# A cached-attention decode block on one core: the last row's second layer in two groups, tail loads first, zero matmuls between

## The chip, the cores and the metric

The kernel runs on one core of a Trainium2 chip. The metric is the device time of one execution in microseconds (us). TensorE is PE in the profile, its weight loads are PEld, VectorE is DVE, ScalarE is ACT, GpSimd is POOL and SyncE, which issues most loads, is SP.

## The reference

Eight rows (one token each, 448 wide) go through attention over a cached window, a dense block with silu, and both once more with the same weights and the same cache:

```python
def _A_ref(x, k_cache, v_cache, wq, wo):
    W = min(4096, max(256, Sk // 4))            # 1024
    q = (x @ wq).reshape(B, Sq, Hq, Dh).transpose(0, 2, 1, 3)   # 16 heads of 256
    k = jnp.repeat(k_cache[:, :, Sk - W:, :], 2, axis=1)        # 8 key heads
    v = jnp.repeat(v_cache[:, :, Sk - W:, :], 2, axis=1)
    p = _softmax(jnp.einsum("bhqd,bhkd->bhqk", q, k) * (Dh ** -0.5), axis=-1)
    o = jnp.einsum("bhqk,bhkd->bhqd", p, v)
    return o.transpose(0, 2, 1, 3).reshape(B, Sq, Hq * Dh) @ wo
...
x = x + _A_ref(_layernorm(x), A_k_cache, A_v_cache, A_wq, A_wo)
x = x + _B_ref(_layernorm(x), B_w1, B_w2)       # silu(x @ w1) @ w2
x = x + _A_ref(_layernorm(x), A_k_cache, A_v_cache, A_wq, A_wo)
x = x + _B_ref(_layernorm(x), B_w1, B_w2)
```

Each row has its own 8 key and 8 value heads of 1024 x 256 in bf16 (512 KB each), 64 MB over all rows.

## The kernel before, in words

Every K and V head of a row is loaded once and serves both layers. It lands in one of 30 slots in SBUF (`load_kv`, L495); the sequence is K of row 0, V of row 0, K of row 1 and so on. SP issues a load as soon as the slot's last reader is done; from the 31st load on that reader is the second layer of a row two places back. The weights come in between: wq (three full chunks, L435, and two 64-partition tails, L429) first, w2 (L453) and wo (L447) after the first row's K, w1 (L441) after the first row's V, with two 64-partition tails of its own (L429).

A row's first layer: DVE turns each K slot in place by 32x32 blocks (`transposes`, L638). PE takes the scores of four key heads at a time (`scores`, L654), so that two passes of 32 matmuls give all 16 heads in one bank. `softmax` (L669 to L683) takes the maximum of each partition on DVE, exchanges it between the partitions that belong to one head by an ACT step (L670), a matmul against a fixed pattern (L671) and a minimum on DVE (L673), then the exp on ACT (L674), a permutation on PE (L676) and a 32x32 turn on DVE (L678). `products` (L689) and, for the last two heads that land, `products_late` (L698) multiply with V; `o_turn` (L711, L715, L719) divides by the sum and turns the result to columns; `wo_rows` (L740) applies wo; `fold` (L746, L528, L531) adds it to the row. `chain(b)` is the dense block (L751 statistics input, L757, L543 for w1, L778 tanh, L798 for w2) and the projection to the second layer's q (L813, L818, L819, L826, L830). The second layer runs `attend2` and `values2` on the slots that are still there.

In the second layer of rows 0 to 6, wo, the dense block and the output are done for all seven rows at once (`final_rows`, L864 to L908). Row 7 goes alone to its end (`final_last`, to L945), after all loads.

The program is a list of tasks with declared reads and writes (`Plan`); the order of the tasks on PE, DVE, ACT and POOL is a table written out in the file (`ORDER`, L13), and SP's order is that of the program text. Each engine takes its tasks strictly in that order and waits by semaphores for tasks of other engines. A load with `via="act"` is issued by ACT ahead of all its tasks.

Of the kernel before, what the change touches and what calls it, by code (L numbers as in the profile page):

```python
# [4 lines left out]
BF16 = mybir.dt.bfloat16  # L5
# [29 lines left out]
    "dve":  # L35
# [14 lines left out]
    "act":  # L50
# [8 lines left out]
    "pool":  # L59
        "0 1 79 130 131 250 219 249 236 378 348 379 365 507 508 477 494 636 606 637 623 765 735 752 766 895 894 864 "  # L60
        "881 993 1024 1023 1010 1108 1125 1162 1218",
}


class Task:
    __slots__ = ("eng", "fns", "dur", "row", "name", "deps", "idx", "end", "sem", "val", "vc", "users", "via")

    def __init__(self, eng, fns, dur, row, name):
        self.eng, self.fns, self.dur, self.row, self.name = eng, fns, dur, row, name
        self.deps = {}  # L70
        self.users = 0
        self.end = None

# [148 lines left out]
def bass_interleave_layers__sliding_block_cached__dense_activation_silu__decode_kernel(  # L222
# [9 lines left out]
    P = 128  # L232
# [833 lines left out]
```

## Time and profile before

| | us |
|---|---|
| median of 3 runs | 235.23 |
| the three runs | 236.98, 235.23, 233.61 |
| the profiled execution | 233.86 |
| its span, first to last instruction | 232.0 |
| PE busy (matmuls) | 161.9 |
| DVE busy | 154.6 |
| ACT busy | 71.8 |
| POOL busy | 22.8 |

The span was executed at a mean granted TensorE clock of 0.963 of full speed. The page divides the span into 40 slices of 5.8 us and gives in each the busy share in tenths; a row of the timeline gives start, length, engine, line, operation, what is written and read, the count of instructions, and in brackets how long the engine had been idle and what released it. HBM read was 77.67 MB.

### The profile page before, as it was taken

How to read it: one execution, taken by the hardware profiler on the slowest of the kernel's cores; microseconds unless marked ns; L12 is line 12 of the kernel's file. 1: busy time of each engine (PE TensorE's matmuls, PEld its weight loads, DVE VectorE, ACT ScalarE, POOL GpSimd, SP SyncE). 2: the span in 40 equal slices, each digit the busy share in tenths (PEclk: the TensorE clock that was granted, in tenths of full speed). 3: DMA queues.
4: the chain of work that ended last, by engine and by line, in shares of the span. 5: the costliest groups of instructions: out<-in, count | busy, mean ns of one | idle time of the engine just before them, and what ended most of it. 6: DMA issues, size and time to landing. Idle time of an engine off the chain costs nothing.

```text
span 232.0 us, 7993 instructions
## 1 busy us (share of the span) xinstructions
PE 161.9 (70%) x3558; PEld 90.8 (39%) x3558; DVE 154.6 (67%) x361; ACT 71.8 (31%) x218; POOL 22.8 (10%) x41
## 2 busy tenths in 40 slices
PE   0000617174777889798697988897987999899883
PEld 0000604022434455345443554454444445444542
DVE  6108999996894796488559935793985599424413
ACT  2000070663103341342243222413622441343241
POOL 1000201003000120030011001010200020000020
PEclk9999999679589999999999988999999999999999
DMA  6999999999999999999999999999999999700000
GB/s 213 296 386 410 383 381 394 405 415 420 403 410 383 411 407 375 381 414 406 353 384 413 408 374 410 386 357 395 412 410 393 386 399 410 284 3 3 3 3 4
DMA packets 22680, 78.19 MB, mean 337 GB/s; under 512 B 2279, under 2 KB 5302, under 8 KB 22262
## 3 DMA queue, kind: packets, MB, share of 16 engines
q1 hardware_dynamic: 22326, 76.93, 85.5%
q10 hardware_dynamic: 320, 0.75, 1.2%
q8 instruction: 28, 0.46, 0.8%
q14 instruction: 6, 0.05, 0.1%
HBM read 77.67 MB, written 0.01 MB: 335 GB/s over the span
## 4 chain that ended last, share of the span: by engine, by line
PE 39%; SPq 20%; DVE 15%; DMA 13%; ACT 8%; issue 3%; DVEq 0%
DMA slot<-in_A_k_cache_dram 13%; SPq L495 11%; PE bank L654 9%; DVE slot L638 8%; SPq L447 7%; PE bank L689 7%; PE pair L740 4%; PE pair L813 3%; PE bank L813 2%; PE pair L798 2%; ACT ot L711 2%; PE bank L826 2%; ACT ot L746 1%; PE pair L528 1%; DVE q1s L669 1%
## 5 line engine op out<-in xcount | busy, mean ns | idle before, releaser
L638 DVE STREAM_TRANSPOSE slot<-slot 128x512 uint32<-128x512 uint32 (+1 forms) x96 | 81.0, 870 | 19.2 <-DMA slot<-in_A_k_cache_dram 18.6
L654 PE MATMUL bank<-slot,qbd 128*16 128x256 bf16 (+1 forms) x1024 | 39.0, 286 | 5.5 <-POOL qbd L625 1.9
L689 PE MATMUL bank<-slot,qbd 128*24 128x512 bf16 (+6 forms) x440 | 34.1, 405 | 3.1 <-DVE qbd L678 2.3
L654 PEld LDWEIGHTS bank<-slot,qbd 128*16 128x16 bf16 (+1 forms) x1024 | 23.4, 88 | 14.3 <-ACT qbd L830 4.3
L762 POOL TENSOR_TENSOR fcols<-fcols 128x1 f32<-128x1 f32 x17 | 9.4, 552 | 87.1 <-ACT fcols L760 79.3
L625 POOL TENSOR_TENSOR qbd<-q1s,fcols 128x256 bf16<-128x256 bf16 x16 | 9.7, 612 | 84.0 <-PE bank L698 37.5
L711 ACT ACTIVATE ot<-bank,q1s 128x512 bf16<-128x512 f32 x16 | 11.0, 686 | 18.7 <-PE bank L689 15.5
L740 PE MATMUL pair<-wo_sb,q1s 128*1 128x449 bf16 x288 | 16.1, 353 | 0.6 <-ACT wo_sb L483 0.4
L830 ACT ACTIVATE qbd<-bank 128x256 bf16<-128x256 f32 x16 | 6.1, 383 | 33.5 <-PE bank L826 33.5
L597 PE MATMUL pair<-slot,wq_sb 128*128 128x16 bf16 x128 | 3.6, 174 | 16.8 <-DVE slot L590 16.8
L689 PEld LDWEIGHTS bank<-slot,qbd 128*24 128x24 bf16 (+6 forms) x440 | 10.1, 93 | 11.6 <-DVE qbd L678 3.7
L669 DVE TENSOR_REDUCE q1s<-bank 128x1 f32<-128x256 f32 x16 | 6.8, 423 | 10.3 <-PE bank L654 10.2
L471 DVE TENSOR_REDUCE slot<-wo_sb 128x6 f32<-128x2688 bf16 x4 | 11.7, 2924 | 0.0
L678 DVE STREAM_TRANSPOSE qbd<-bank 128x256 bf16<-128x256 bf16 x16 | 7.5, 466 | 6.3 <-PE bank L676 6.1
L479 ACT ACTIVATE slot<-w_sb 128x448 bf16<-128x448 bf16 x6 | 3.5, 576 | 24.4 <-DMA w_sb<-in_B_w_dram 24.2
L670 ACT ACTIVATE q1s<-fcols,q1s 128x4 f32<-128x4 f32 x16 | 4.7, 296 | 19.1 <-DVE q1s L669 19.1
L674 ACT ACTIVATE qbd<-bank,q1s 128x256 bf16<-128x256 f32 x16 | 7.6, 472 | 8.8 <-DVE q1s L673 8.6
L813 PE MATMUL pair<-wq_sb,q1s 128*1 128x256 bf16 x256 | 9.8, 293 | 0.6 <-ACT q1s L804 0.6
L751 DVE TENSOR_TENSOR q1s<-pair,fcols 128x5 bf16<-128x5 f32 x17 | 2.7, 159 | 11.2 <-PE pair L531 11.1
L597 PEld LDWEIGHTS pair<-slot,wq_sb 128*128 128x128 bf16 x128 | 3.5, 104 | 16.9 <-DVE slot L590 16.9
L671 PE MATMUL bank<-q1s,quad 128*128 128x4 f32 x32 | 6.1, 262 | 5.5 <-ACT q1s L670 5.3
L798 PE MATMUL pair<-w_sb,q1s 128*1 128x449 bf16 x112 | 7.4, 353 | 3.6 <-DVE q1s L786 3.4
(158 smaller groups left out, 240.0 us busy)
## 6 DMA issues: line engine op xcount, KB each, us to landing
slot<-in_A_k_cache_dram SPq DMA_DIRECT2D x64, 512.0 KB, 8.7
slot<-in_A_v_cache_dram SPq DMA_DIRECT2D x64, 512.0 KB, 9.7
wo_sb<-in_A_wo_dram SPq DMA_DIRECT2D x4, 896.0 KB, 15.0
wq_sb<-in_A_wq_dram SPq DMA_DIRECT2D x3, 1024.0 KB, 10.6
w_sb<-in_B_w_dram SPq DMA_DIRECT2D x1, 1568.0 KB, 19.8
w_sb<-in_B_w_dram SPq DMA_DIRECT2D x1, 1344.0 KB, 17.4
wq_sb<-in_A_wq_dram ACTq DMA_DIRECT2D x2, 256.0 KB, 6.0
w_sb<-in_B_w_dram ACTq DMA_DIRECT2D x1, 128.0 KB, 9.9
```

Source lines behind the costliest of these rows:

```text
L447: dma(lambda e, g=g: e.dma_start(wo_sb[:, 4 * g * PW:4 * (g + 1) * PW].rearrange("p (h n) -> p h n", n=PW)[:, :, R0:M1], A_wo[1024 * g:102 ...
L471: dve(lambda e, rows=rows, s=s: e.tensor_reduce(s, rows[:, :, R0:M1].rearrange("p c (a n) -> p c a n", a=2), AX.X, ALU.add, negate=True), ...
L495: dma(lambda e: e.dma_start(slots[s][:, :].rearrange("p (u d) -> p u d", d=DH), cache[b, kvh, S0:SK, :].rearrange("(p u) d -> p u d", p=P) ...
L625: pool(lambda e, k2=k2: e.tensor_tensor(qdata(0, k2), q1s[:, b, 64 * k2:64 * k2 + 64].rearrange("p (n r) -> p n r", r=2).unsqueeze(3) .bro ...
L638: dve(lambda e, v=v: e.transpose(v, v), keys, keys, 0.15 + n / 2 / 950, b, ("KW%d" if n > 1024 else "KT%d") % k)
L654: fns.append(lambda e, w=w, j=j, kv=kv, cb=cb, par=par: e.matmul(sc[32 * j:32 * j + up_to, 0:256], w, kv, start=(cb == 0 and par == 0), st ...
L689: pe([lambda e, t=t: e.matmul(bank[ob][32 * t:32 * t + m, :], pT_sb[L][:, 64 * t:64 * t + m], v[:, 512 * t:512 * t + 512], start=True, sto ...
L711: act(lambda e: e.activation(o_t, src[1], ACTF.Copy, scale=sm[b][:, 4 * L + 3:4 * L + 4]), bk(src[0]) + [("sm", b, L, 3)], okey, 0.62, b, ...
L740: fns.append(lambda e, i=i, w=w, c0=c0: e.matmul(bank[XB][32 * (i % 4):32 * (i % 4) + 1, c0:c0 + D + 1], oT[:, oT_col(i):oT_col(i) + 1], w ...
L762: pool(lambda e: e.tensor_tensor(rhalf, var4, nhalf, ALU.pow), ["var4", "nhalf"], ["rhalf"], 0.54, b, "pow" + name)
L798: fns.append(lambda e, f=f, w=w, c0=c0: e.matmul(bank[XB][32 * (f % 4):32 * (f % 4) + 1, c0:c0 + D + 1], hT[b][:, f:f + 1], w, start=(f < ...
L813: pe([lambda e, j=j, c=c, qh=qh, k2=k2, h=h, n=n: e.matmul(qh[32 * j:32 * j + 1, :], xbt[b][:, xcol(c, k2):xcol(c, k2) + 1], view(wq_sb[:] ...
```

## The change

Four things are edited, and all four order tables are new.

1. *Tails first.* `load_tails()` is called before `load_wq()`, so that the tails of wq and w1 stand ahead of the full chunks of wq. Of each pair of tails one goes on SP's queue, the other on ACT's.
2. *Table first.* In ACT's order the load of the activation tables (task 2) moves from the last row's part to the first place.
3. *Zero matmuls.* `warm(b, n)` adds n rounds of four matmuls with a weight column of zeros and 512 columns of wq, one in each column group, into the bank of the first layer's products. There are 8 rounds ahead of row 0's products, and 12, 5, 4, 4, 4, 4, 4 and 3 declared after the products of rows 0 to 7; the first stands at the head of PE's order, and all read wq.
4. *Two groups.* The second layer of row 7 is done for key heads 0 to 3 and 4 to 7 separately, each with its own score bank, softmax, products, `o_turn` and half of wo. The maximum of a group is exchanged between partitions by two 32x32 turns and a small minimum on DVE in place of the ACT and PE steps. The batch of seven rows uses another bank for w1 (`WB8`).

```diff
+    WARM = (8, 12, 5, 4, 4, 4, 4, 4, 3)
...
-                    [(key, 3 + h)], 64 * n * 2, "%st%d" % (key, h), rate=400e3, via="act")
+                    [(key, 3 + h)], 64 * n * 2, "%st%d" % (key, h), rate=370e3, via=("sp", "act")[h])
...
     def load_wq():
...
-            if c == 0:
-                load_tails()
...
-    def softmax(b, L):
+    def softmax(b, L, part=None):
+        sb, n, m = (SC[L], L, L) if part is None else (part[0], part[1], 1 - part[1])
...
+            mt, mg = part[2][:, 0:64].bitcast(F32), part[2][:, 64:80].bitcast(F32)
+            bias = mt[:, 0:1]
+            dve(lambda e: e.tensor_reduce(mt[:, 0:1], x, AX.X, ALU.max, negate=True), bk(sb), [("mt", n)] + part[3], 0.41,
+                b, "max%d" % L)
+            dve(lambda e: e.transpose(mt, mt), [("mt", n)], [("mt", n)], 0.21, b, "mT")
+            dve(lambda e: e.tensor_reduce(mg, mt.rearrange("p (n q) -> p n q", q=4), AX.X, ALU.min), [("mt", n)],
+                [("mg", n)] + part[3], 0.17, b, "mg")
+            dve(lambda e: e.transpose(mt.rearrange("p (n q) -> p n q", q=4), mg.unsqueeze(2).broadcast_to([P, 8, 4])),
+                [("mg", n)], [("mt", n), K[1]], 0.21, b, "mb")
...
+    def warm(b, n):
+        for k in range(n):
+            pe([lambda e, i=i: e.matmul(bank[OB[0]][32 * i:32 * i + 1, :], zero_b, wq_sb[:, 512 * i:512 * i + 512],
+                                        start=True, stop=True, tile_position=(0, 32 * i), skip_group_check=True)
+                for i in range(4)], WQ_R + ["cols0"], bk(OB[0]), 0.054, b, "fill")
...
-        XB8, YB8, WB8 = SC[0], OB[0], LB[0]
+        XB8, YB8, WB8 = SC[0], OB[0], SC[0]
...
+    load_tails()
     load_wq()
...
+        if b == 0:
+            warm(b, WARM[0])
         for kvh in range(HKV - LATE):
             products(b, 0, kvh, OB[0])
         o_turn(b, 0, (OB[0], bank[OB[0]][:]), ot[:], ["ot"], 2 * LATE, H, oT1[b], [("oT1", b, 0)], "0")
+        warm(b, WARM[b + 1])
...
     def attend2(b):
+        if b == LAST:
+            s = slot_of[LAST - 1, "v", 2]
+            for k2, sb in enumerate((SC[1], OB[1])):
+                scores(b, 1, k2, sb)
+                softmax(b, 1, (sb, 1 - k2, slots[s][:, 128 * k2:128 * k2 + 128], slot_key(s)))
+            return
...
+        s = slot_of[LAST - 1, "v", 2]
+        for k2, ob in enumerate((SC[1], OB[1])):
+            for kvh in range(4 * k2, 4 * k2 + 4):
+                products_late(b, kvh, bank[ob][:, 0:256], bk(ob), k2, "PVL")
+            o_turn(b, 1 - k2, (ob, bank[ob][:, 0:256]), slots[s][:, 512:768] if k2 else ot[:, 0:256],
+                   slot_key(s) if k2 else ["ot"], 8 - 8 * k2, 16 - 8 * k2, oT2[b], [("oT2", k2)], "L")
+            wo_rows(b, range(16 * k2, 16 * k2 + 16), oT2[b], [("oT2", k2)], "woL", NCH - 4)
+        fold(b, 1.0, [], "L")
```

In the new orders the tasks of rows 1 to 6 keep nearly their sequence on PE, with the zero rounds between them; DVE's order at the start and in row 0 differs more. The last row's groups stand on PE as: scores of both, half of w1 and the statistics of the batch, products of group one with the permutation of group two between, products of group two, then the turns and wo of both. ACT has the two copies (L711 before) one after the other and then the two turned copies (L719 before).

More of the change, by code (lines that the diff above doesn't have):

```diff
@@ L639, in transposes, with scores @@
                 ("KW%d" if n > 1024 else "KT%d") % k)
-    def scores(b, layer, k2):
-        sc = bank[SC[layer]]
+    def scores(b, layer, k2, sb=None):
+        sb = SC[layer] if sb is None else sb
+        sc = bank[sb]
         q = qbd[layer][:]
@@ L657, in scores @@
             pe(fns, [x for j in range(4) for x in slot_key(slot_of[b, "k", 4 * k2 + j])] + [("pad", layer)] + QB(layer, k2),
-               bk(SC[layer]), 0.0285, b, "S%d.%d" % (layer, k2))
-    def softmax(b, L):
-        lb = bank[LB[L]]
-        x = bank[SC[L]][:, 0:256]
+               bk(sb), 0.0285, b, "S%d.%d" % (layer, k2))
+    def softmax(b, L, part=None):
+        sb, n, m = (SC[L], L, L) if part is None else (part[0], part[1], 1 - part[1])
+        lb = bank[LB[n]]
+        x = bank[sb][:, 0:256]
@@ L664, in softmax @@
         px = lb[:, 256:512]
-        mneg, bias, acc, rlr = (sm[b][:, 4 * L + i:4 * L + i + 1] for i in range(4))
-        mq = sm[b][:, 8 + 4 * L:12 + 4 * L]
-        K = [("sm", b, L, i) for i in range(5)]
+        mneg, bias, acc, rlr = (sm[b][:, 4 * n + i:4 * n + i + 1] for i in range(4))
+        mq = sm[b][:, 8 + 4 * n:12 + 4 * n]
+        K = [("sm", b, n, i) for i in range(5)]
         mx, lr = lb[:, C_MX:C_MX + 4], lb[:, C_L:C_L + 1]
-        dve(lambda e: e.tensor_reduce(mneg, x, AX.X, ALU.max, negate=True), bk(SC[L]), [K[0]], 0.41, b, "max%d" % L)
@@ L670, in softmax @@
-        act(lambda e: e.activation(mq, sel4, ACTF.Copy, scale=mneg), [K[0], "sel4"], [K[4]], 0.2, b, "mq%d" % L)
-        pe(lambda e: e.matmul(mx, quad[:], mq, start=True, stop=True, skip_group_check=True), [K[4], "quad"], bk(LB[L]),
-           0.2, b, "mx%d" % L)
-        dve(lambda e: e.tensor_reduce(bias, mx, AX.X, ALU.min), bk(LB[L]), [K[1]], 0.15, b, "mb%d" % L)
-        act(lambda e: e.activation(e_sb[L], x, ACTF.Exp, bias=bias, scale=1.0, accum_out=acc),
-            bk(SC[L]) + [K[1]], EK[L] + [K[2]], 0.6, b, "exp%d" % L)
@@ L676, in softmax @@
-        pe(lambda e: e.matmul(px, perm[:], e_sb[L], start=True, stop=True),
-           EK[L] + PERM + QM * L, bk(LB[L]), 0.13, b, "perm%d" % L)
-        dve(lambda e: e.transpose(view(pT_sb[L], 0, [(64, 4), (1, 2), (2, 32)]), px.bitcast(BF16)[:, 1:512:2]),
-            bk(LB[L]), PT[L], 0.44, b, "turn%d" % L)
+        if part is None:
+            dve(lambda e: e.tensor_reduce(mneg, x, AX.X, ALU.max, negate=True), bk(sb), [K[0]], 0.41, b, "max%d" % L)
+            act(lambda e: e.activation(mq, sel4, ACTF.Copy, scale=mneg), [K[0], "sel4"], [K[4]], 0.2, b, "mq%d" % L)
+            pe(lambda e: e.matmul(mx, quad[:], mq, start=True, stop=True, skip_group_check=True), [K[4], "quad"],
+               bk(LB[n]), 0.2, b, "mx%d" % L)
+            dve(lambda e: e.tensor_reduce(bias, mx, AX.X, ALU.min), bk(LB[n]), [K[1]], 0.15, b, "mb%d" % L)
+        else:
+            mt, mg = part[2][:, 0:64].bitcast(F32), part[2][:, 64:80].bitcast(F32)
[7 more added lines that the diff above has]
+                [("mg", n)], [("mt", n), K[1]], 0.21, b, "mb")
@@ L680, in softmax @@
+        act(lambda e: e.activation(e_sb[m], x, ACTF.Exp, bias=bias, scale=1.0, accum_out=acc),
+            bk(sb) + [K[1]], EK[m] + [K[2]], 0.6, b, "exp%d" % L)
+        pe(lambda e: e.matmul(px, perm[:], e_sb[m], start=True, stop=True),
+           EK[m] + PERM + QM * m, bk(LB[n]), 0.13, b, "perm%d" % L)
+        dve(lambda e: e.transpose(view(pT_sb[m], 0, [(64, 4), (1, 2), (2, 32)]), px.bitcast(BF16)[:, 1:512:2]),
+            bk(LB[n]), PT[m], 0.44, b, "turn%d" % L)
         pe([lambda e, t=t: e.matmul(lr[32 * t:32 * t + 32, :], lsel[:], acc, start=True, stop=True,
@@ L681, in softmax @@
                                     tile_position=(0, 32 * t), skip_group_check=True) for t in range(4)],
[L682 to L683 removed]
+           [K[2], "lsel"], bk(LB[n]), 0.05, b, "l%d" % L)
+        dve(lambda e: e.reciprocal(rlr, lr), bk(LB[n]), [K[3]], 0.15, b, "rl%d" % L)
     def products(b, L, kvh, ob):
@@ L998, in values2 @@
     def values2(b):
-        end = HKV if b < LAST else HKV - LATE
-        for kvh in range(end):
-            products(b, 1, kvh, OB[1])
-            freed.add((b, "v", kvh))
-        pump()
-        o_turn(b, 1, (OB[1], bank[OB[1]][:]), ot[:], ["ot"], 2 * (HKV - end), H, oT2[b], [("q1s", b)], "1")
-        if b == LAST:
-            for i in range(0, 4 * end, 8):
-                wo_rows(b, range(i, i + 8), oT2[b], [("q1s", b)], "woL")
-            late(b, 1, oT2[b], "oT2")
-            wo_rows(b, range(NCH - 4 * LATE, NCH), oT2[b], [("oT2", b, 7)], "woL7")
-            fold(b, 1.0, [], "L")
+        if b < LAST:
+            for kvh in range(HKV):
+                products(b, 1, kvh, OB[1])
+                freed.add((b, "v", kvh))
+            pump()
+            o_turn(b, 1, (OB[1], bank[OB[1]][:]), ot[:], ["ot"], 0, H, oT2[b], [("q1s", b)], "1")
+            return
+        s = slot_of[LAST - 1, "v", 2]
[6 more added lines that the diff above has]
+        fold(b, 1.0, [], "L")
     pump()
```

20 lines of the change are left out of this document (9 added, 11 removed), and 86 rows, old and new, of the table ORDER.

## The prediction

> **What bounds the kernel now.** I read the page's 40 slices first, then busy time by stretch (columns: stretch, its length, busy time and instruction count of PE, weight load, DVE, ACT and POOL, granted clock, DMA share, GB/s).
>
> ```profile
> PEclk9999999679589999999999988999999999999999
> DMA  6999999999999999999999999999999999700000
> GB/s 213 296 386 410 383 381 394 405 415 420 403 410 383 411 407 375 381 414 406 353 384 413 408 374 410 386 357 395 412 410 393 386 399 410 284 3 3 3 3 4
> ```
>
> ```profile
> 2.00:6.00 4.00, 0.38 (x5) 0.28 (x5) 3.16 (x18) 1.47 (x2) 0.00 (x0) 1.00 0.96 329
> 6.00:9.00 3.00, 0.48 (x12) 0.40 (x12) 1.12 (x6) 0.05 (x1) 0.00 (x0) 1.00 1.04 242
> 9.00:13.00 4.00, 0.00 (x0) 0.00 (x0) 0.00 (x0) 0.00 (x0) 0.00 (x0) 1.00 1.03 346
> 13.00:17.00 4.00, 0.00 (x0) 0.00 (x0) 0.00 (x0) 0.00 (x0) 0.00 (x0) 1.00 0.99 400
> 56.00:86.00 30.00, 21.77 (x440) 11.75 (x444) 22.79 (x43) 8.67 (x27) 3.11 (x6) 0.89 1.02 404
> 86.00:96.00 10.00, 8.34 (x187) 5.11 (x180) 5.99 (x15) 2.57 (x9) 0.55 (x1) 1.00 0.97 375
> 111.00:119.00 8.00, 6.16 (x133) 3.65 (x135) 3.29 (x9) 2.79 (x8) 0.02 (x1) 1.00 0.99 352
> 86.00:201.00 115.00, 98.14 (x2157) 54.73 (x2153) 81.68 (x174) 38.27 (x115) 12.03 (x21) 0.99 1.01 393
> ```
>
> The span falls in two: 203 us (35 slices of 5.8) in which the DMA engines are hardly ever idle, then 29 us without loads, which is one row's dependent chain. No engine is full in the first part; the loads are. So the time is the moment when the last V slot lands, plus the tail. When it lands, and why the stream isn't always at 404 GB/s, is in the SP queue: who made it wait (us in total, times, longest), then the last two V loads, and the loads from 60 to 80.
>
> ```profile
> SPq L495 <- PE bank L654: 56.9, 15, 11.5
> ```
>
> ```profile
> L495 SPq DMA_DIRECT2D slot<-in_A_v_cache_dram x2: 327/380/434, 195.8 to 196.1; - x2
> ...
> DMA to landing us min/median/max: 6.0/6.4/6.9
> ```
>
> ```profile
> L495 SPq DMA_DIRECT2D slot<-in_A_v_cache_dram x3: 327/328/434, 68.6 to 79.9; - x3
> ...
> DMA to landing us min/median/max: 4.5/7.0/9.6
> ```
>
> The last load lands at 196.1 + 6.9 = 203.0, so the tail is 232.0 - 203.0 = 29.0. SP waits for the score matmuls of layer 2 (L654), which free the K slots; once for 11.5 us, up to the first gate at 68.6. The load that lands soonest after its issue does so in 4.5 us: a queue of three or four transfers, since a 512 KB slot takes 1.3 at 404. Behind such gates the stream sags: (404-375)/404 x 10 = 0.7 us lost in 86 to 96, (404-352)/404 x 8 = 1.0 in 111 to 119, and 3.1 over the 115 us from 86.
>
> **Part 1: tails first.** Before, 736 KB of 64-partition loads on ACT's queue (columns: count, KB each, us to landing) mix with the three 1 MB loads of wq on SP's.
>
> ```profile
> wq_sb<-in_A_wq_dram ACTq DMA_DIRECT2D x2, 256.0 KB, 6.0
> w_sb<-in_B_w_dram ACTq DMA_DIRECT2D x1, 128.0 KB, 9.9
> w_sb<-in_B_w_dram ACTq DMA_DIRECT2D x1, 96.0 KB, 11.0
> ```
>
> ```profile
> L435 SPq DMA_DIRECT2D wq_sb<-in_A_wq_dram x3: 369/422/851, 1.2 to 2.1; - x3
> ...
> DMA to landing us min/median/max: 6.8/10.6/13.0
> ```
>
> wq is complete at 2.1 + 13.0 = 15.1. Against 400 GB/s the stretches lose 3 x (400-242)/400 = 1.2 us, 4 x (400-346)/400 = 0.5 and 4 x (400-329)/400 = 0.7, together 2.4. Afterwards the tails go two and two on SP and ACT ahead of wq, and mix mostly with each other. If they move at the worst rate seen, 736 KB take 3.1 us at 242 against 1.9 at 400: a loss of 1.2 in place of 2.4. I take 1.2 us off every later landing. Bounds: 2.4 if nothing is lost, 0 if the same packets are as slow in any order, and 0.8 worse, because SP issues wq behind two more issues of some 0.4 us. [...] The 242 while two queues mix speaks for a cost of mixing, which an order can change.
>
> **Part 2: table first, and a zero round at the head of PE.** The table load moves ahead of an ACT wait that has slack in both orders: nothing. But the first PE instruction now waits for all five wq loads, at 13.9 by part 1. Behind it in PE's queue stand the transposition of x, the statistics and q1; DVE, ACT and POOL wait for those. Before, that early chain had come to its DVE step by 7.4:
>
> ```profile
> 7.23 0.17 DVE L564 TENSOR_SCALAR slot<-bank 128x8 f32<-128x8 f32 x1
> ```
>
> after which DVE waited for K, transposed, and only then let q1 go:
>
> ```profile
> 17.63 2.53 DVE L638 STREAM_TRANSPOSE slot<-slot 128x1024 uint32<-128x1024 uint32 x2 [10.23 <-DMA slot<-in_A_k_cache_dram]
> ```
>
> ```profile
> 23.87 3.58 PE L597 MATMUL pair<-slot,wq_sb 128*128 128x16 bf16 x128 [16.84 <-DVE slot L590]
> ```
>
> The chain is at most 7.4 long, so it ends by 13.9 + 7.4 = 21.3, and the cover is K transposes. In DVE's new order the last piece ahead of q1 stands behind four wide transposes and a half (4.5 x 1.27, from about 16, with the waits for K and small pieces: near 24), before behind three, at 23.9. So q1 keeps its time and DVE is ahead by one and a half. Cost 0; without that cover up to 1, taken up by DVE's row sums.
>
> **Part 3: 48 zero rounds.** Each is four matmuls of 512 columns in four column groups. The nearest rows are L689 with few weight columns, alone and three sets in a row:
>
> ```profile
> 200.50 0.39 PE L689 MATMUL bank<-slot,qbd 128*24 128x512 bf16 x4
> ```
>
> ```profile
> 205.33 0.82 PE L689 MATMUL bank<-slot,qbd 128*12 128x512 bf16 x12
> ```
>
> A round is (0.82-0.39)/2 = 0.21 us, alone 0.39; 48 are 10 us of PE. Twenty lie in row 0 and its chain, where PE waits for DVE and DMA and the granted clock falls to a half (the 6, 7, 5 and 8 of the slices). The last q projection of row 0, right ahead of the scores that open the gate at 68.6, and the same in row 7:
>
> ```profile
> 63.58 1.92 PE L813 MATMUL bank<-wq_sb,q1s 128*1 128x512 bf16 x16
> ```
>
> ```profile
> 191.96 1.08 PE L813 MATMUL bank<-wq_sb,q1s 128*1 128x512 bf16 x16
> ```
>
> That is 0.84, and the other half of the projection, as many columns, lies in the same dip: 1.7 together. At full clock, and with part 1, the gate opens some 3 us sooner while the loads move by 1.2: the queue is one or two transfers deeper. I count the sag of 86 to 96 as gone and 0.4 of the next, 1.1 us. Bounds: 3.1 (all of it) and 0. The other 28 rounds, three to five a row, stand mostly before a matmul that waits: the statistics for DVE, the two softmax steps for ACT, the fold for the row copy. For the last, in row 1:
>
> ```profile
> 85.04 0.29 PE L528 MATMUL pair<-cols,ot 128*128 128x1 bf16 x5 [0.73 <-ACT ot L746]
> ```
>
> Two rounds, 0.42, fit into 0.73. I charge 0.3 for a few that don't fit. The bound is two rounds of each row's chain uncovered, 0.42 in each of seven rows, 2.9 us; below nothing is excluded beyond the clock gain, as they compute nothing that is used. [...]
>
> **Part 4: the last row in two groups** (and the batch's w1 in another bank, no cost). Now its last scores end at 216.70 and the exp starts at 218.18:
>
> ```profile
> 214.88 1.82 PE L654 MATMUL bank<-slot,qbd 128*16 128x256 bf16 x56
> ```
>
> ```profile
> 218.18 0.47 ACT L674 ACTIVATE qbd<-bank,q1s 128x256 bf16<-128x256 f32 x1 [0.67 <-DVE q1s L673]
> ```
>
> Group one has 24 of these 56 and ends near 215.7. Its maximum (256 columns, taken like the exp's 0.47) is followed on DVE by three small pieces, in place of an ACT, a PE and a DVE step. At their shape the trace has none; the bounds are L564's 0.17 for 128x8 and a quarter of a wide transpose's 1.27, 0.32, for far more columns; I take 0.2, near the row of like size. With one piece of the batch between, DVE is free at 217.0, so group two's maximum starts 0.25 late and its exp at 218.05 against 218.18: no earlier. Its products then stand behind group one's four sets of eight 256-wide matmuls, of which two take 0.61 now, and one copy is 0.69, half as wide 0.47:
>
> ```profile
> 221.03 0.61 PE L698 MATMUL bank<-slot,qbd 128*7 128x256 bf16 x16
> ```
>
> ```profile
> 221.25 0.69 ACT L711 ACTIVATE ot<-bank,q1s 128x512 bf16<-128x512 f32 x1 [2.50 <-PE bank L689]
> ```
>
> ```profile
> 221.84 0.47 ACT L711 ACTIVATE qbd<-bank,q1s 128x256 bf16<-128x256 f32 x1
> ```
>
> ```profile
> 222.67 1.70 PE L740 MATMUL pair<-wo_sb,q1s 128*1 128x449 bf16 x32
> ```
>
> With 0.21 for each further set, both groups are through at about 221.05 against 221.25, the copy at 221.5. ACT copies both groups before it turns either, so wo starts at 221.8 against 222.67, and its 32 matmuls still take 1.70: 0.87 earlier. Later the residual matmuls come to stand before w1's second half and give back some 0.25. Gain 0.6. Bounds: 1.5 if half of wo (0.85) were done in time, and 0.1 worse if the six small pieces cost 0.32.
>
> **Sum.** 232.0 - 1.2 - 1.1 + 0.3 - 0.6 = 229.4 of span; the profiled execution has 233.86 for a span of 232.0, so 1.9 is added: 231.3. Its 233.86 lies 1.4 below the median of 235.23; I leave the forecast at its level, as clock dips are my best guess at what the other runs have more of.
>
> **Rivals.**
> - *Deep queue.* The gates of all rows open in time and the whole 3.1 us of sag goes, with 2.0 from the tails: 232.0 - 2.0 - 3.1 - 0.6 + 1.9 = 228.2, down to 227. For: the sag comes behind gates. Against: a row's own chain from last V to gate hardly changes.
> [...]
> - *Zero rounds delay the gates.* The queue is only three transfers deep, so once a row's chain is about 0.6 us longer, every later landing is later by the excess. Price: four rounds on the path at 0.39 are 1.6 a row, so 7 x (1.6 - 0.6) = 7 us, hence 239 to 241. For: PE is busy 98.14 of 115, idle is scarce. Against: the rounds stand in front of waits.
>
> **Numbers.** From no change a measurement of this kernel can tell about 2%, here 4.7 us: faster is under 230.5, slower over 239.9. Forecast 0.53, of 228.8 to 233.5, a little under half of it faster (0.24). Deep queue 0.22, all faster. Gates 0.12, the same. Zero rounds 0.13, slower. So 0.46, 0.41 and 0.13. For 8 in 10 I reach down to 227 and up to 236, which leaves out the slow case and a little below.
>
> **What would show it.** Part 1: wq complete near 13.9, first K transpose some 1.2 earlier. Part 3: granted clock 9 in slices 8 to 12, the first gate's issue near 65 to 66, 404 GB/s through 86 to 96. Part 4: wo of the last row starting 5.1 us after the end of its last score matmul (now 222.67 - 216.70 = 6.0). Wrong if the last V slot lands at 203 or later, or the tail after it stays at 29.

## The result, and the profile after

In 20 runs beside 20 of the kernel before, the changed kernel took 233.2 us (median of all) against 235.82. The ratio is 0.988, with a 95% interval of 0.984 to 0.992: 2.6 us gained, a difference that is real and under 2%. The profiled execution took 230.15 us for a span of 228.4; it is the lowest of the 20, so the two profiles, 3.7 us apart, overstate the gain. Executions over 1.5% longer than the fastest of the same kernel are left out of all ratios, and two profiles below that are such executions (without rounds, and tails alone) have no marks in the tables.

Four marks divide a span: the landing of the first K slot, the issue of the first V load that waits for a slot (the first gate), the landing of the last V slot, and the end.

| us | before | after | difference |
|---|---|---|---|
| first K slot lands | 16.3 | 14.8 | -1.5 |
| from there to the first gate | 52.3 | 52.1 | -0.2 |
| from there to the last V slot | 134.4 | 133.4 | -1.0 |
| tail | 29.0 | 28.0 | -1.0 |

The page's 40 slices (of 5.7 us now):

```profile
PEclk9999999999999999999999999999999999999999
DMA  6999999999999999999999999999999999700000
GB/s 175 413 406 407 382 380 395 411 414 417 405 400 369 377 408 403 396 408 407 406 406 408 402 378 411 408 392 395 410 409 385 380 408 406 307 3 3 0 6 1
```

The clock row has no dip left, in row 0 or later, which does not yet say that the matmuls were fast (see Part 3 below). The stream still has dips: behind the eighth, slices 13, 14, 24, 31 and 32 stand at 369 to 385 GB/s. By stretch, with the columns as in the prediction:

```profile
6.00:9.00 3.00, 0.00 (x0) 0.00 (x0) 1.25 (x10) 0.00 (x0) 0.00 (x0) 1.00 1.00 415
9.00:13.00 4.00, 0.00 (x0) 0.00 (x0) 0.00 (x0) 0.00 (x0) 0.00 (x0) 1.00 1.00 414
...
56.00:86.00 30.00, 26.01 (x575) 13.64 (x579) 22.56 (x48) 9.35 (x29) 4.56 (x8) 1.00 1.02 393
86.00:96.00 10.00, 9.64 (x201) 5.06 (x193) 5.29 (x14) 3.07 (x9) 0.02 (x1) 1.00 1.02 398
111.00:119.00 8.00, 6.98 (x147) 3.93 (x139) 3.96 (x9) 3.12 (x10) 0.61 (x1) 1.00 1.03 407
86.00:201.00 115.00, 103.63 (x2268) 56.80 (x2264) 80.81 (x171) 38.25 (x115) 11.51 (x20) 1.00 1.00 392
```

The start is clean: 415 and 414 where 242 and 346 stood. Of the rest, 86 to 96 and 111 to 119 have recovered (375 and 352 before), but 56 to 86 has fallen (404 before), and 86 to 201 as a whole is the same, 392 against 393. The sag has moved, not gone. SP's longest waits (us in total, times, longest), and the last two V loads:

```profile
SPq L496 <- PE bank L656: 59.5, 12, 8.9
```

```profile
L496 SPq DMA_DIRECT2D slot<-in_A_v_cache_dram x2: 328/380/432, 193.1 to 193.5; - x2
...
DMA to landing us min/median/max: 6.0/6.4/6.9
```

SP waits for the score matmuls (L656 now) as long as before, 59.5 us against 56.9. The last slot lands at 193.5 + 6.9 = 200.4. PE's rows of the tail (start, length):

```profile
212.90 1.83 PE L656 MATMUL bank<-slot,qbd 128*16 128x256 bf16 x56
...
219.62 1.69 PE L754 MATMUL pair<-wo_sb,q1s 128*1 128x449 bf16 x32
```

and ACT's two exps, one for each group:

```profile
215.06 0.47 ACT L688 ACTIVATE qbd<-bank,slot 128x256 bf16<-128x256 f32 x1 [1.67 <-DVE slot L686]
...
216.08 0.47 ACT L688 ACTIVATE qbd<-bank,slot 128x256 bf16<-128x256 f32 x1 [0.45 <-DVE slot L686]
```

The last score matmul ends at 214.73, and wo starts 4.89 later; before it was 222.67 - 216.70 = 5.97.

### The profile page after: what moved, and what is told of

Same layout as the page of the kernel before. It is cut to its first block, busy times and chain, and to the rows that moved or that the text cites. A ratio compares the mean times of both kernels' runs of the same rounds, so it can differ in the third digit from the quotient of the medians.

```text
span 228.4 us, 8452 instructions
## 1 busy us (share of the span) xinstructions
PE 173.0 (76%) x3779; PEld 94.1 (41%) x3779; DVE 157.2 (69%) x369; ACT 71.4 (31%) x218; POOL 22.8 (10%) x41
## 4 chain that ended last, share of the span: by engine, by line
PE 46%; DVE 31%; DMA 10%; ACT 6%; issue 4%; SPq 2%; DVEq 0%; ACTq 0%
DVE slot L639 12%; DMA slot<-in_A_k_cache_dram 10%; PE bank L656 10%; PE bank L703 7%; DVE slot L472 7%; PE pair L754 6%; PE bank L781 2%; PE pair L833 2%; ACT ot L760 2%; PE bank L675 2%; PE bank L846 2%; PE bank L712 2%; PE bank L833 2%; PE pair L529 2%; PE pair L818 1%
## 5 line engine op out<-in xcount | busy, mean ns | idle before, releaser
L656 PE MATMUL bank<-slot,qbd 128*16 128x256 bf16 (+1 forms) x1024 | 40.9, 285 | 5.1 <-DVE slot L639 2.0
L703 PE MATMUL bank<-slot,qbd 128*24 128x512 bf16 (+6 forms) x416 | 31.1, 393 | 3.5 <-DVE qbd L692 3.3
L656 PEld LDWEIGHTS bank<-slot,qbd 128*16 128x16 bf16 (+1 forms) x1024 | 23.2, 87 | 16.7 <-ACT qbd L850 4.0
L781 PE MATMUL bank<-wq_sb,cols 128*1 128x512 bf16 x192 | 19.6, 416 | 13.9 <-DMA wq_sb<-in_A_wq_dram 13.9
L754 PE MATMUL pair<-wo_sb,q1s 128*1 128x449 bf16 x288 | 17.2, 353 | 1.1 <-DVE wo_sb L475 0.8
L850 ACT ACTIVATE qbd<-bank 128x256 bf16<-128x256 f32 x16 | 6.1, 384 | 33.5 <-PE bank L846 33.5
L725 ACT ACTIVATE ot<-bank,q1s 128x512 bf16<-128x512 f32 (+1 forms) x16 | 10.8, 673 | 16.4 <-PE bank L703 11.1
L692 DVE STREAM_TRANSPOSE qbd<-bank 128x256 bf16<-128x256 bf16 x17 | 8.0, 473 | 8.2 <-PE bank L690 7.9
L781 PEld LDWEIGHTS bank<-wq_sb,cols 128*1 128x1 bf16 x192 | 4.2, 82 | 15.4 <-issue 13.9
L833 PE MATMUL pair<-wq_sb,q1s 128*1 128x256 bf16 x256 | 8.9, 275 | 0.3 <-DVE q1s L765 0.3
L712 PE MATMUL bank<-slot,qbd 128*7 128x256 bf16 (+7 forms) x192 | 8.6, 283 | 0.6 <-DVE qbd L692 0.6
L833 PE MATMUL bank<-wq_sb,q1s 128*1 128x512 bf16 x128 | 8.8, 390 | 0.0
## 6 DMA issues: line engine op xcount, KB each, us to landing
wo_sb<-in_A_wo_dram SPq DMA_DIRECT2D x4, 896.0 KB, 14.6
```

Of the source, the lines that this page charges most:

```text
L656: fns.append(lambda e, w=w, j=j, kv=kv, cb=cb, par=par: e.matmul(sc[32 * j:32 * j + up_to, 0:256], w, kv, start=(cb == 0 and par == 0), st ...
L703: pe([lambda e, t=t: e.matmul(bank[ob][32 * t:32 * t + m, :], pT_sb[L][:, 64 * t:64 * t + m], v[:, 512 * t:512 * t + 512], start=True, sto ...
L712: pe([lambda e, t=t, a=a: e.matmul(o[32 * t:32 * t + m, :], pT_sb[n][:, 64 * t + a:64 * t + a + m], v[:, 512 * t + DH * a:512 * t + DH * a ...
L725: act(lambda e: e.activation(o_t, src[1], ACTF.Copy, scale=sm[b][:, 4 * L + 3:4 * L + 4]), bk(src[0]) + [("sm", b, L, 3)], okey, 0.62, b, ...
L754: fns.append(lambda e, i=i, w=w, c0=c0: e.matmul(bank[XB][32 * (i % 4):32 * (i % 4) + 1, c0:c0 + D + 1], oT[:, oT_col(i):oT_col(i) + 1], w ...
L781: pe([lambda e, i=i: e.matmul(bank[OB[0]][32 * i:32 * i + 1, :], zero_b, wq_sb[:, 512 * i:512 * i + 512], start=True, stop=True, tile_posi ...
```

## The experiments

Twelve kernels, each timed 6 or 12 times beside the kernel before. They take parts out of the changed kernel or put parts into the kernel before. "Old orders" are the tables of the kernel before, "new orders" those of the changed kernel without the places of the zero rounds. Marks are of one profile each; a star stands where the granted clock was at a half for some 3.4 us inside the tail or just ahead of it.

| kernel | ratio to before (95%) | first K | to first gate | to last V | tail |
|---|---|---|---|---|---|
| before | 1 | 16.3 | 52.3 | 134.4 | 29.0 |
| changed kernel | 0.988 (0.984-0.992) | 14.8 | 52.1 | 133.4 | 28.0 |
| 1 no rounds | 0.995 (0.991-1.000) | | | | |
| 2 later rounds doubled | 1.000 (0.996-1.005) | 16.0 | 52.1 | 136.8 | 28.6 |
| 3 old tails | 0.988 (0.982-0.993) | 15.7 | 52.1 | 133.2 | 28.5 |
| 4 one group | 0.995 (0.991-0.999) | 14.9 | 52.1 | 133.5 | 30.5* |
| 5 rounds of row 0 only | 0.992 (0.987-0.996) | 15.0 | 52.1 | 132.9 | 30.2* |
| 6 rounds of later rows only | 1.000 (0.996-1.004) | 15.1 | 53.7 | 133.6 | 28.7 |
| 7 before + new orders | 1.011 (1.007-1.015) | 15.9 | 56.0 | 132.9 | 31.2* |
| 8 before + groups | 0.994 (0.990-0.999) | 15.8 | 53.7 | 134.7 | 27.9 |
| 9 before + tails | 0.999 (0.994-1.004) | | | | |
| 10 before + tails + groups | 0.992 (0.988-0.996) | 14.8 | 53.4 | 136.0 | 28.3* |
| 11 as 10 + rounds of row 0 | 0.988 (0.983-0.993) | 14.8 | 53.3 | 134.2 | 27.2 |
| 12 as 11, old tails | 0.999 (0.993-1.004) | 15.8 | 52.1 | 135.9 | 27.3 |

**1. No zero rounds.** The rounds add nothing to the output.

```diff
-    WARM = (8, 12, 5, 4, 4, 4, 4, 4, 3)
+    WARM = (0, 0, 0, 0, 0, 0, 0, 0, 0)
```

> The changed kernel without its 48 zero rounds (WARM all 0, their places in PE's order closed); nothing else differs. Theory 1 (the forecast: the rounds raise TensorE's clock in row 0, the first gate opens sooner, the queue is deeper): the granted clock falls to a half again in slices of row 0, the first gated V load is issued at 69 to 70 instead of 66.9, and the last V slot lands 1.1 later, near 201.5; the time is about 1 us above the changed kernel, 0.992 to 0.993 of the kernel before. Theory 2 (the stream is broken by the 16 KB instruction packets that the trace shows on queue q8, each some 1.05 us on one DMA engine, and not by late gates): the clock falls too, but the last V slot lands within 0.5 of 200.4, with one or two packets of 16 KB fewer in the stream; the time stays at 0.986 to 0.990. Rival 3 (the rounds stand in the way of the gates): the last slot lands 1 to 3 us sooner, 0.975 to 0.984.

0.9954 against 0.9881: the rounds are worth 0.7 +- 0.6% here, near theory 1's time. But the granted clock did not fall in row 0, as theories 1 and 2 had it; its only dip ahead of the end is at 162.2. The matmuls there were slow all the same (1.92 us for the sixteen of 512 columns at 67.88). Where the gate stands is read from runs 5 to 7.

**2. The later rounds doubled.**

```diff
-    WARM = (8, 12, 5, 4, 4, 4, 4, 4, 3)
+    WARM = (8, 12, 10, 8, 8, 8, 8, 8, 6)
```

> The changed kernel with the 28 zero rounds of rows 1 to 7 doubled, each round twice in its place; row 0 keeps its 20. PE gets 28 x 0.21 to 0.39 = 6 to 11 us more work. Theory 1 (rounds lie in waits): at most 0.3 to 0.6 us later, 0.989 to 0.991 of the kernel before. Theory 2 (instruction packets break the stream): 224 more instructions on PE (a matmul and a weight load each of 112) are about one packet more, up to 1.1 us on one DMA engine: last V slot at 200.4 to 201.5, 0.988 to 0.993. Rival 3 (rounds are on the path to the gates): 0.84 to 1.6 a row beyond what the queue forgives, the last V slot 3 to 7 us later, 1.00 to 1.02.

1.2 +- 0.6% slower than the changed kernel, as rival 3 has it in time and in place: the stretch from the first gate to the last V slot is 3.4 us longer at a clock of 9 in all 40 slices. In rows 1 to 6, the time from the landing of a row's last V slot to the next row's gate sums to 91.8 us, against 87.0 in the changed kernel: 0.8 a row. So a row's chain can pace the stream, and 28 further rounds no longer fit beside it.

**3. The tails as before**, on ACT's queue behind the first chunk of wq.

```diff
-                    [(key, 3 + h)], 64 * n * 2, "%st%d" % (key, h), rate=370e3, via=("sp", "act")[h])
+                    [(key, 3 + h)], 64 * n * 2, "%st%d" % (key, h), rate=400e3, via="act")
...
                 [("wq", c)], P * HD * 2, "wq%d" % c, rate=420e3)
+            if c == 0:
+                load_tails()
...
-    load_tails()
     load_wq()
```

> The changed kernel with the tails loaded as before: all four on ACT's queue, declared behind the first chunk of wq. Theory 1 (two queues with small rows beside wq cost DMA time): wq is complete at 15.0 instead of 13.5, the first K slot lands at 16.3, 242 GB/s or so in 6 to 9 us, and the last V slot lands 1.2 to 1.5 later; 0.994 to 0.995 of the kernel before. Rival (the stream is paced by the gates, so that a later start is taken up): wq and the first K as late, but the last V slot within 0.5 of the changed kernel's; 0.986 to 0.990. Rival 2 (the same bytes cost the same in any order): wq complete at 13.5.

wq was complete at 14.4 and the first K slot landed 0.9 later than in the changed kernel; the last V slot landed 0.7 later in this profile, but the time was the same, 0.9876. See runs 9 to 12.

**4. One group in the last row**, with the old sequence of the tail.

```diff
     def attend2(b):
-        if b == LAST:
-            s = slot_of[LAST - 1, "v", 2]
-            for k2, sb in enumerate((SC[1], OB[1])):
-                scores(b, 1, k2, sb)
-                softmax(b, 1, (sb, 1 - k2, slots[s][:, 128 * k2:128 * k2 + 128], slot_key(s)))
-            return
         for k2 in range(2):
             scores(b, 1, k2)
...
```

> The changed kernel with layer 2 of the last row in one group as before (and the order of the tail from the kernel before, from the batch's statistics on); tails, table and the 48 rounds stay. Theory 1 (two groups bring 0.6 to 1.0): the last V slot lands where it does in the changed kernel, 200.4 give or take 0.5, and the tail behind it is 29.0 instead of 28.0; 0.991 to 0.993 of the kernel before. Rival (the shorter tail came from the clock or from the order of the rest, not from the groups): the tail is 28.0 to 28.3, 0.988.

0.7 +- 0.6% slower, with the stream unchanged (133.5): the groups do it, together with the order of the tail that goes with them in every run here. The tail is longer than theory 1 had it, 30.5 and not 29.0. PE's rows of its tail, and the window from 215 to 222, in which the granted clock fell to 0.76 on the mean:

```profile
213.33 1.81 PE L656 MATMUL bank<-slot,qbd 128*16 128x256 bf16 x56
...
218.39 2.31 PE L691 MATMUL bank<-slot,qbd 128*28 128x512 bf16 x20
...
222.34 1.70 PE L742 MATMUL pair<-wo_sb,q1s 128*1 128x449 bf16 x32
```

```profile
215.00:222.00 7.00, 5.84 (x104) 2.84 (x96) 2.42 (x8) 1.95 (x6) 1.49 (x1) 0.76 0.01 2
```

From the last score matmul (215.14) to wo it takes 7.20 instead of 5.97, because the products run at half clock: their last sixteen of 256 columns take 1.08 us, 0.61 before. Run 7, without a dip at that place, has 5.97. All kernels with two groups have 4.89.

**5 and 6. The rounds of row 0 alone, and those of rows 1 to 7 alone.**

```diff
-    WARM = (8, 12, 5, 4, 4, 4, 4, 4, 3)
+    WARM = (8, 12, 0, 0, 0, 0, 0, 0, 0)
```

> The changed kernel with the 20 zero rounds of row 0 and its chain alone; the 28 of rows 1 to 7 are taken out. Theory 4 (the rounds of row 0 bring the gain, since they make PE's matmuls short some 18 us sooner and so open the first gate; those of later rows only cost PE time, as their doubling cost 1.2% of the time): the first gated V load is issued 52.1 after the first K slot's landing as in the changed kernel, the last V slot lands 0 to 2.8 sooner, and the time is 0.976 to 0.988 of the kernel before. Rival (the later rounds hold the clock, and all are needed): a dip of the granted clock in rows 1 to 7, 0.990 to 0.996.

```diff
-    WARM = (8, 12, 5, 4, 4, 4, 4, 4, 3)
+    WARM = (0, 0, 5, 4, 4, 4, 4, 4, 3)
```

> The changed kernel with the 28 zero rounds of rows 1 to 7 alone; the 20 of row 0 are taken out, the first PE instruction is the transposition of x again. Theory 4: matmuls stay at 0.6 us or more until about 70 us, the first gated V load is issued 55 after the first K slot's landing (52.1 in the changed kernel) and the queue runs empty around 72 to 80, so the time is 0.995 to 1.003 of the kernel before, at least as late as without any rounds (0.9954). Rival (later rounds bring the gain): 0.986 to 0.990.

Run 5 gave 0.9915, between theory 4's range and the rival's: 0.3 +- 0.6% above the changed kernel. Its gate stands at 52.1 as theory 4 says, but taking the later rounds out gains nothing: they cost nothing to begin with, and only their doubling does. Run 6 gave 1.0002, and the gate went to 53.7, not to 55. So the rounds of row 0 are worth 1.2 +- 0.5% with the later ones present, 0.4 +- 0.6% without them; the later ones are worth nothing that these runs can tell (+0.3 and -0.5%, +- 0.6 each).

In run 6 the sixteen 512-wide matmuls took 1.91 us, slow as expected, but in a dip of the clock that began at 59.6; by 54 its matmuls had become fast without any rounds. The first sixteen matmuls of wo in run 6, and the same in run 7 below, which has the same order up to there and no rounds:

```profile
54.02 0.93 PE L755 MATMUL pair<-wo_sb,q1s 128*1 128x449 bf16 x16 [1.11 <-DVE wo_sb L476]
```

```profile
55.16 1.67 PE L741 MATMUL pair<-wo_sb,q1s 128*1 128x449 bf16 x16 [1.11 <-DVE wo_sb L475]
```

So when the matmuls of row 0 become fast differs between executions of the same order, and the gate of a single profile moves with it.

**7. The kernel before with the new orders alone.**

```diff
 ORDER = {
     "pe":
-        "69 74 86 87 88 89 92 136 137 161 138 139 148 149 150 151 154 157 196 197 198 159 199 200 201 208 203 205 "
+        "69 74 86 87 88 89 92 136 94 137 138 139 148 149 161 150 151 154 157 196 197 159 198 199 200 201 208 209 "
...
```

> The kernel before with nothing but the new orders of rows 0 to 7 up to the batch's statistics, and the table first; tails, softmax and tail order as before, no zero rounds. If the orders carry nothing (the forecast, which gave them no term): 0.997 to 1.003 of the kernel before, tail 29.0, first gate 52.3 after the first K slot. If the orders are part of the gain: 0.990 to 0.996. If the orders alone make row 0 worse and were made for the rounds: first gate 54 to 55 after the first K slot, 1.000 to 1.010.

1.1 +- 0.4% slower, and the first gate 3.7 us later than before: the third expectation, and somewhat beyond it in both. The page's slices, and PE's rows from row 0's products to the gate:

```profile
PEclk9999999999999999999999999999999999799999
DMA  6999999999986999999999999999999999400000
GB/s 216 315 399 408 382 380 398 410 412 414 408 327 228 404 369 412 352 407 405 406 408 408 409 385 410 408 378 366 417 412 401 401 404 403 175 3 3 3 3 4
```

```profile
50.16 1.04 PE L690 MATMUL bank<-slot,qbd 128*32 128x512 bf16 x8 [3.29 <-DVE qbd L679]
...
67.62 1.92 PE L814 MATMUL bank<-wq_sb,q1s 128*1 128x512 bf16 x16
...
70.01 1.84 PE L655 MATMUL bank<-slot,qbd 128*16 128x256 bf16 x48
```

The same rows of the changed kernel:

```profile
48.34 1.04 PE L703 MATMUL bank<-slot,qbd 128*32 128x512 bf16 x8 [3.29 <-DVE qbd L692]
...
63.00 1.08 PE L833 MATMUL bank<-wq_sb,q1s 128*1 128x512 bf16 x16
...
65.03 1.86 PE L656 MATMUL bank<-slot,qbd 128*16 128x256 bf16 x48
```

And of the kernel before:

```profile
45.70 1.47 PE L689 MATMUL bank<-slot,qbd 128*32 128x512 bf16 x12 [2.30 <-DVE qbd L678]
...
66.91 1.89 PE L654 MATMUL bank<-slot,qbd 128*16 128x256 bf16 x48
```

In all three, the products wait for DVE's turn of the exp (L678, L679, L692). In run 7 these two sums of w2 stand ahead of the turn, 4.0 us together, beside sums of wo:

```profile
38.22 1.98 DVE L472 TENSOR_REDUCE slot<-w_sb 128x4 f32<-128x1792 bf16 x1
...
44.67 2.01 DVE L472 TENSOR_REDUCE slot<-w_sb 128x4 f32<-128x1792 bf16 x1
...
49.65 0.45 DVE L679 STREAM_TRANSPOSE qbd<-bank 128x256 bf16<-128x256 bf16 x1
```

Before, the sums of w2 stood behind the turn and only sums of wo ahead of it:

```profile
42.28 2.93 DVE L471 TENSOR_REDUCE slot<-wo_sb 128x6 f32<-128x2688 bf16 x1
45.20 0.45 DVE L678 STREAM_TRANSPOSE qbd<-bank 128x256 bf16<-128x256 bf16 x1
...
49.61 3.94 DVE L471 TENSOR_REDUCE slot<-w_sb 128x4 f32<-128x1792 bf16 x2
```

So the products start 34.3 us after the first K slot lands; before they started at 45.70, 29.4 after it. The changed kernel starts them as late, 33.5 after it; its gate is early because the way from there to the gate's matmuls takes only 16.7 us, where run 7 takes 19.9 and the kernel before 21.2: the sixteen 512-wide matmuls take 1.92 in run 7 and 1.08 in the changed kernel, at a 9 in both clock rows, and each sixteen of wo 1.67 and 0.93. Around the late gate the stream runs dry (327 and 228 GB/s in slices 12 and 13). From the gate on, this kernel's stream is as short as the changed kernel's, 132.9.

**8, 9 and 10. The kernel before with the groups alone** (run 4's edit the other way round), **with the tails alone** (run 3's the other way round), **and with both.**

> The kernel before with layer 2 of the last row in two groups, and the tail's order that goes with it, and nothing else: old tails, old orders before the tail, no rounds. Theory 1 (the groups shorten the tail by 0.6 to 1.0, in any case): tail 28.0 to 28.4 against 29.0, 0.993 to 0.997 of the kernel before. Theory 5 (by the runs so far the groups are worth 0.7% or 1.7 us): 0.992 to 0.994, tail 27.3 to 28.0. Rival (the tail gains nothing by itself): 1.000, tail 28.8 to 29.2.

> The kernel before with the tails loaded first, two on SP's and two on ACT's queue, and nothing else. Theory 1 (the earlier start carries through to the last V slot): wq complete at 13.5 to 13.8, unless one DMA engine lags, first K slot 1.2 to 1.5 sooner than 16.3, last V slot at 201.5 to 202, 0.993 to 0.995 of the kernel before. Rival (other delays of single DMA engines and the gates take it up, as the run with the old tails in the changed kernel has it at 0.9876): wq and K as early, but 0.998 to 1.002.

> The kernel before with the tails first and the two groups of the last row, with its own orders ahead of the tail and no zero rounds. If the parts add up: 0.994 (groups alone) less 0 to 0.5% for the tails, 0.989 to 0.994, and the changed kernel's 0.988 needs neither its rounds nor its new orders. If the orders and rounds of the changed kernel bring something together: 0.994 or more.

The groups alone give 0.6%, with a tail of 27.9. The tails alone give nothing that the runs can tell, and the two together 0.8 +- 0.4%. Up to the tail, run 8 is the program of the kernel before, and yet its first gate came 1.4 us later (53.7 and 52.3): by that much at least the mark of one profile is uncertain.

**11 and 12. Run 10 with 20 rounds set into the old orders of row 0, and the same with old tails.**

```diff
-    WARM = (0, 0, 0, 0, 0, 0, 0, 0, 0)
+    WARM = (8, 12, 0, 0, 0, 0, 0, 0, 0)
```

> As the kernel with tails first and two groups alone, with 20 zero rounds in row 0 and its chain besides, set into the orders of the kernel before (two each behind q1, the first selection, the last scores and the maximum of row 0; twelve in the chain, four of them behind the first half of w1). Theory 4 (warm matmuls in row 0 open the first gate): matmuls of row 0 near 0.4 us and no half clock from 40 to 66, first gated V load 49.5 to 50.5 after the first K slot's landing (52.3 before, 52.1 in the changed kernel), a queue some 2 us deeper behind it, last V slot 0.5 to 2 sooner, 0.982 to 0.988 of the kernel before. Rival (a gate that opens earlier than 52 buys nothing, since the stream's gaps are delays of single DMA engines): the gate as early, but 0.988 to 0.994, the same as without rounds.

> As the run with 20 rounds set into the old orders, but with the tails loaded as before: so the kernel before with two groups and row 0's rounds alone. Theory 1 (an earlier start carries through): wq complete at 14.4 to 15.0, last V slot 0.7 to 1.5 later than with the tails first, 0.992 to 0.995 of the kernel before. Rival, by three comparisons so far (tails alone 0.9992; the changed kernel with old tails 0.9876; groups without and with the tails 0.9942 and 0.9921): the tails are worth 0.2 us or so, and the time is 0.986 to 0.991, with intervals between landings that are too long in 2 to 3 us behind 16 KB packets for about 5 us in total, as in the other runs.

Run 11 is as fast as the changed kernel, 0.988, without the new orders and with 20 rounds. But theory 4 missed its mark: the gate came 53.3 us after the first K slot, not 50, and the granted clock was at a half from 40.5 to 47.3 us and again from 64.4. PE's rows of run 11, and DVE's:

```profile
61.22 1.08 PE L834 MATMUL bank<-wq_sb,q1s 128*1 128x512 bf16 x16
65.03 0.61 PE L847 MATMUL bank<-qbd,band 128*128 128x64 bf16 x4 [2.73 <-DVE qbd L840]
```

```profile
62.68 0.71 DVE L640 STREAM_TRANSPOSE slot<-slot 128x512 uint32<-128x512 uint32 x1 [1.25 <-DMA slot<-in_A_k_cache_dram]
63.31 0.42 DVE L839 STREAM_TRANSPOSE pair<-pair 128x256 f32<-128x256 f32 x1
```

The projection is done early, at 62.3. Its turn on DVE (L839) stands behind a transpose of K that waits for the load, and PE then waits 2.73 us. In this order faster matmuls can't move the gate ahead of the landing of row 1's K. Run 12 gave 0.999, above both of its expectations, with a last V slot 1.45 us later, as its theory 1 had it, and 1.1 +- 0.7% slower than run 11: the only one of four comparisons in which the tails show. The four (runs 3, 9, 10 against 8, and 12 against 11) give +0.05, -0.1, -0.2 and -1.1%, weighted by their intervals -0.3 +- 0.3%, or 0.6 +- 0.7 us gained.

No run was faster than the changed kernel beyond the intervals.

## Why the prediction came out as it did, step by step

**The sum and the level.** The forecast took 2.6 us off the profiled execution of before; the medians differ by 2.6. That is luck: its parts were not that close, and their errors cancel. It missed the median by 1.9 us (231.3 against 233.2), and the step that failed there is "I leave the forecast at its level": 233.86 was a lucky execution. From the median of three it would have been 235.23 - 2.6 = 232.6, from that of the 20 later executions of before 235.82 - 2.6 = 233.2.

**The bound** held in both kernels: the loads until the last V slot, then a chain without loads.

**Part 1** forecast wq at 13.9 and got 13.5, with the rate of 6 to 9 up from 242 to 415 GB/s. All five kernels with old tails have 242 to 313 there, the nine with tails first 380 to 426: the start did lose time as the row said. As a term of the time, 1.2 was probably too large. wq was complete at 15.0, 14.4, 14.6, 14.6 and 14.6 in the five kernels with old tails, and the profiled execution of before was the slowest of these; the seven profiles with tails first in the table have 13.5 to 14.7, on the mean 13.8. That is 0.8 to 0.9 sooner, and the time shows 0.6 +- 0.7. The times don't exclude a term of 0; the 242 and 415 show that order and queues together did change the rate at the start.

**Part 2** held. q1 starts where it did (23.87 before), its wait for wq covered by DVE:

```profile
23.97 3.58 PE L598 MATMUL pair<-slot,wq_sb 128*128 128x16 bf16 x128 [7.51 <-DVE slot L591]
```

**Part 3** failed in its mechanism. The clock row is full in slices 8 to 12, as forecast, but a full row was no sign of fast matmuls: until about 52 us they were as slow in the changed kernel as in run 7 (the products above take 1.04 us in both), in spite of the rounds ahead of them. And the step "the gate opens some 3 us sooner while the loads move by 1.2" did not come: the gate came 1.7 us sooner, at 66.9 and not 65 to 66, and all but 0.2 of that is the start. What the forecast left out is the new orders, to which it gave no term. Without the rounds of row 0 they put the first gate at 56.0 (run 7) or 53.7 (run 6); the rounds bring it back to 52.1 in five kernels of five (the changed one and runs 2 to 5). So the rounds repay a cost of the change itself. In the old order they don't open the gate sooner either, since DVE waits there for K (run 11).

The 1.0 us that the stream did gain belongs to the orders too, as far as the profiles show it. From the first gate to the last V slot, the six kernels in the table with new orders and no doubled rounds take 132.9 to 133.6 us, with 0, 20, 28 or 48 rounds, and the five with old orders 134.2 to 136.0. Which of the moved tasks does it wasn't tried. So without the rounds the new orders cost 1.4 (run 6) to 3.7 us (run 7) in row 0 and give back some 1.8 later; with the rounds, the 1.8 stays. From the first K slot to the last V slot that makes 185.0 to 185.6 us for new orders with the rounds of row 0, 187.3 and 188.9 without these, and 186.7 to 189.4 for old orders. This rests on one profile a kernel; the times agree in sign for the orders alone (+1.1 +- 0.4%), but run 11, with old orders, was as fast as the changed kernel.

The sag itself was misread in part. If the short stops described at the end are counted, the profile before loses 6.3 us in intervals between landings that are over 0.1 us too long, and 5.1 of these follow an instruction packet; the changed kernel loses 5.5 and 5.1. So late gates had little more than 1 us to give there, and the bound of 3.1 took a loss for theirs that stayed.

The 0.3 us charged for rounds that don't fit is not contradicted, since the first 28 cost nothing that an interval of 0.6% (1.4 us) shows. The rival *Zero rounds delay the gates* came true at twice the number.

**Part 4** had the right mechanism and too small a size. wo starts 4.89 us after the last score (5.1 forecast), which is 1.08 sooner, and the 0.25 that later pieces were to give back is not there: from wo's start to the last copy of the output it is 6.2 us in both. The times give 0.65 +- 0.3% for the groups (runs 4, 8, and 10 against 9), 1.5 us. In the pair of profiles the tail is 0.97 shorter: 1.08 less from the groups, 0.7 more from the last slot to the last score matmul (13.7 before, 14.4 after), and 0.6 less from the last copy of the output to the end (3.1 and 2.5). That last 0.6 is not the groups': runs 4 and 7, with one group, have 2.5 too. What else the groups bring in the times is open: of the profiles in the table, one of the three with one group has a half clock among the products (run 4, 1.2 us) and none of the nine with two, which are too few to tell.

**The rivals.** *Deep queue* is out: 86 to 201 moved no faster than before. That the gates pace the stream, so that an earlier start only makes SP wait longer, had a chance of 0.12 and would have given 232.0 - 0.6 + 1.9 = 233.3. It was nearer the truth than that chance says, though 233.3 was met by luck, from the level of a lucky execution. When the chains of rows 1 to 6 grow by 4.8 us in sum (run 2), the stream is 3.4 longer; when they shrink from 90.6 before to 87.0 after, it is 1.0 shorter. The sum of the chains does not settle the stream alone: run 7 has 90.1 and a stream of 132.9, run 11 has 87.3 and 134.2. That the loads themselves fill the time once the chains are short is argued from these pairs and not shown.

**What doesn't add up.** Taken one by one, the effects are -0.3% (tails), -0.65% (groups), +1.1% (orders) and -0.7% (rounds): -0.6% in sum, where the change has -1.2 +- 0.4%. In the presence of tails and groups the orders cost only 0.3 or 0.4 +- 0.7% (run 1 against 10, run 5 against 11), which would close the gap, but the intervals are too wide to call that an interaction.

## What to carry to other kernels

An order table is a change in itself: price it as a part, by the first wait that each moved task now stands behind, and time the new order without the parts it was made for. Where the loads and a dependent chain take nearly the same time in every step, reckon that speeding up one gains only in part: here chains 4.8 us longer in sum went with a stream 3.4 longer, and chains 3.6 shorter with one 1.0 shorter. Filler work was free only up to a point: 28 rounds cost nothing that the times show, and 28 more 1.2%. Put a forecast on the median of the runs, take only the differences from the profile, and take a mark from more than one profile: the same order had its gate 1.4 us apart in two.

## What the runs showed of the hardware

**A full clock row did not mean fast matmuls.** In run 7 the clock row has 9 through row 0, yet sixteen matmuls of 512 columns took 1.92 us up to 69.5 us of the span, and 1.08 in the changed kernel at 63.0. Within the changed kernel, with a 9 in the row at both places, the four matmuls of a zero round took 0.60 us at 33.85 and 0.39 at 52.15. Its trace has clock records from 51.77 us on, that of the kernel before from 38.51; ahead of them the row has 9 as well, so in these two profiles it does not show the slow start, and the durations do.

**The clock also fell behind busy stretches.** The dips of 3.4 us at 137.5 us in the kernel before (a granted clock of 0.50 up to 140.9), at 218.4 in run 4 and at 74.6 in run 11 each follow 3.4 us in which PE was busy for 68 to 73%, with no idle stretch over 0.6 us in the 6.8 us ahead. What set them off is open.

**The stream's short stops follow instruction packets.** The changed kernel's page lists, beside the loads (queue, kind: packets, MB, share of 16 engines):

```profile
q8 instruction: 29, 0.48, 0.9%
```

These are 16 KB each, one every 6 or 7 us, and each takes mostly some 1.05 us of one DMA engine, while a slot counts here as landed with the last of the 16 parts that the trace has of its load. Slots mostly land 1.28 us apart. Some of the longer intervals of the changed kernel, from the trace:

```
packet starts   slot lands   interval too long by
 79.46           82.15        1.18
110.15          112.33        0.73
130.23          133.34        0.75
157.67          160.66        0.48
```

In all fourteen profiles, 170 intervals between 56 and 206 us are over 0.1 us too long; some 125 of them end 1.9 to 3.3 us after such a packet starts, where some 21% would by chance. They hold some 72 of the 103 us lost: 5.1 us a kernel, the same with and without the change. If the packets are the cause, that is about their price in this stream. That it is the packets and not something in step with them wasn't tried.

**One late part in sixteen held up the slots behind it.** In run 2, fifteen of the sixteen parts of wq's last chunk were in at 13.52 us and the last at 14.69; each of the next six K slots landed with its last part 1.16 to 1.21 us behind the fifteenth. In the two slots after these it was 0.41. With the same loads, wq was complete at 13.54 in the changed kernel.
